# POOL masks the exponentials of a chunk-selected attention by an index select instead of a product with a triangle, under newly arranged lists

## The chip, the cores and the metric

The kernel runs on one core of one Trainium2 chip. The metric is the device time of one execution in microseconds, taken as the median of several runs. Engines are named as in the profile: PE (matrix products), DVE (vector), ACT (activation), POOL (GpSimd), SP (which here only issues DMAs).

## What is computed

Two steps in one program: attention in which each query looks only into the six best of its chunks of 32 keys, and then a two-layer network over all 3072 tokens. The reference, cut to what matters (B 4, H 8, S 768, D 64):

```python
k_min, k_max = min and max of k over each chunk of 32 keys
ub = sum(maximum(q * k_min, q * k_max), axis=-1)          # bound of a chunk, per query
ub = where(query's chunk >= chunk, ub, -1e9)
top_chunks = argsort(ub)[..., -6:]
mask = (key's chunk in top_chunks) & (query >= key)       # causal inside the chunks too
attn = softmax(where(mask, q @ k.T / sqrt(D), -1e9))
x = (attn @ v) as (3072, 512)
h = x @ w_in                                              # 512 -> 2048
g = where(h > 0, h, exp(minimum(h, 0)) - 1)
out = g @ w_out                                           # 2048 -> 512
```

## The kernel before

The work is recorded first and emitted afterwards. Every step (`g.op(name, engines, emit, reads, writes)`) is recorded as an operation with the engines that may do it and a function that emits its instructions. There are 2118 recorded operations, of which 1948 are emitted. Then one written list, `ORDER`, says in which order they are emitted and on which engine: three characters an entry, the engine (P PE, A ACT, D DVE, G POOL, S SP) and two digits for the operation's number. A second list, `PLACES`, says for each buffer, when it first appears, which of its class's slots it gets. So each engine runs its own entries strictly in the list's order, and a reused slot makes its new writer wait for its old readers. SP's entries are the DMAs, and these too are issued strictly in order.

The work comes in units of one batch and one half of the sequence (384 queries), eight in all; the first two units are built from the first and second quarter tiles of batches 0 and 1 together. In each unit, for each of four pairs of heads (`r`):

- `prep`: q and k are loaded (`ldk`, `ldq`), transposed on PE (`kT`, `qT`, line 543, line 402 for the paired units), copied out of PSUM (`kt`, `qt`) and into the operands of the score product (`ka`, `qa`); v is cast (`v`); chunk minima and maxima go to `kst`. For batches 2 and 3, and in the kernel's list these steps lie inside the work of earlier units, minima and maxima come from a contiguous load `ldc` into the one buffer `kc` (lines 480 to 501), and the k rows come transposed by DMA (`kd`). For batches 0 and 1 chunk-row indicators (`ec`) are copied by DMA from `econst` into the score operand.
- `select`: the bounds `ub` on PE (line 592), then on DVE transpose, largest eight, compare, transpose (lines 603 to 620), and `mk` copies the resulting rows into the operand, so that the score product itself adds a large negative number to keys of chunks that were not chosen.
- `attend`: for each step of key blocks a score product `sc` (line 782), the exponential `ex` on ACT (lines 797 and 801) into `pt`, and for the block or blocks on the diagonal the causal mask `tri` (line 814) on DVE or POOL. Then the products with v, `pv` (line 833), whose operand has a column of ones for the sum; `rcp` and `on` (lines 636 and 646) divide; the result is transposed (`px` on PE, line 669, and `xt`; or `xd` by DMA for batches 2 and 3) into `xt`, the network's input.
- `mlp`: for each of 16 blocks of 128 hidden columns a product `h` (line 851), `e` (exponential, ACT, line 858), `m` (minus one, POOL or DVE, line 860), `g` (maximum and minimum, DVE, line 864); then for each tile of 128 tokens 16 products into `o` (line 875, 893 for the last tile), a copy `oe` and the store `out`.

The list weaves the network of one unit between the attention of later ones. The weights w_in and w_out are loaded and cast to bf16 by POOL's DMA queue (`w_in0` to `w_in2`, `w_out0` to `w_out3`).

The causal mask before is one product a step. The `tri` tile holds ones on and above the diagonal; a step whose packed exponentials hold two diagonal blocks (at columns 0 and 384 of 512) is masked by one instruction over both:

```python
view = ap(pt)[:, :, PAD:PAD + 512].rearrange("p h (x w) -> p h x w", w=P)[:, :, ::3, :]
```

Here `h` is the two heads of the pair, so a single block is 128 x 256 elements, a double one 128 x 512, in bf16. There are 48 such masks, 18 on POOL and 30 on DVE; another 8, of line 740, belong to the paired units and are not touched.

Of the kernel before, what the change touches and what calls it, by code (L numbers as in the profile page):

```python
# [9 lines left out]
AOT = mybir.AluOpType  # L10
# [34 lines left out]
Pm-Pn6G2EAn7GbsGmGPn2Gn8D2pG2rAm+Dn0D14D0GAn3Dn4P2wPmWA2xA2yS2RP2JA2KDn5D2zPmSPmODn9Dn1AmXAmTD2L  # L45
GmYPnaGmHDmZAmPP3lAnbGmIA2FDmQDmUPmKAmLDmVD3nD3mA2MD3pGncPnGG2HPniA2AG07GmMA1fPnCG2SAnjD3oPnuD3q
D3rPnmDmRDmNG3tPneAnHA3sGnkDndAnvGnIP3HDnlAnDPnqGnwA3IDnJP41PnyDnxAnrA3uGnEDnFP3JP3+AnfPnQDnsS2k
A3KDntD2NAnnS3fG3LP2XA42P38PnRS2mA40GmJAnzA2GDnoD2ZDnpD2YP4lGngPnKPnXA4mD3vDnhA2+A30D43D3cP4DA4E
P4FG3ePnYA4GGnAD3aA3dD39D2-D31P4jD4HP3gG3bP33PnSS32S4+A34D35PnLA3hA4kD3iG3kS2TDnBP3wD4nS2VG2lG36
D3xG3jS50PnZPn-A2nD3yD3zA37S4-D3APnMPnTD3BD3CS4YD3GA3EG3FP3NDnUP4OP4MS4XS4ZP3MD3DP48P45A4PA4NP44  # L50
G2UG2WP4aD3ODn+D3PP4IP4JA4bP3SPnNA49D46D47A3TD4cS7UP3QD4QAnOP4sP4uP4dA3RP4eP4oS7SA4tP4pD4fP5rG3U
D4gA4vP4RD4KD4LP4SP4hA5sP5QS7WD4TD4UP3VP3WA5RD4qP5fP4VD3XD3YA5gS7RP5ED4rG4wP4xA4WP4yD5SP3ZA5FD4z
P58D4AA5iS57P5kD5aA4iP4BA4CG7VS53P5JD3-P5xD59G5TG5uA5cS55D5BA5oA5NPolPoJD5mA5GD5KPo5S5wAoKD5zS8l
PoxD5yGoLAo6SaND5LA5IPo9A5tDoMSo0G5bPodGo7AomD5lS51AoyG5MPohDo8G5nAoaSnPGonPoRA5OScZGobDooAoePoF
D7TA5hGofAoSPopDocG5AA5jGozDogPo1AoGGoTSnVDoAAoqPoBGoHDoUS7NAoiGorA5DPotDoIS7OAo2GojDosP5VAouGo3
DokA5HGovDo4A5UG5PDowA5vPoNAoCG5dD5XPp1A52G7XD5WAoOD5ZGoDPp2A5qGoPA5eD5YPpePpfD5-SnWPp7D5+SaHPp8
DoEA60G61DoQPpgD63A56DaOP66P6gA67P64DaQP6cP6iA65Pp3D62A6dDaPA6jP6mP68A6hP6lD5pP6aDaRP6eA6nPp9A69
D54SaSG6oA6fP6BP6xD6kPoVA6bS7MA6CP6vA6yS7YP6qA6wP6HS7PP6pAoWP6zA6IS7QPoZD6rGoXD6sA6AG5CP6JDoYAo-
P6tScRP6MGbmP6ND6uA6KP7bGo+P7cP76A6OP6-Dp0PphA77D6LA7dD6PShFScXG7eDaTP6FA6+Pp4ApiA6GP6DA6EP72P70
P78P6RDp5A71A79DaUP6QDaVA73P7CP74A75P6YA6ZP7xP7zA7yA7ADaWP7ZD7aD6SSb3P6WA6XPpaApbP7DSpjSp6G7BP8g  # L60
A8hD7-D81D6TD7+P7rP7lP7fP7gP7tP89P7pD8iA7EG7FD7hD7iD8aD8bG8kG8jP7vP8yD8zA7mA7sA7qA7uP7nA7oA7wP8m
# [24 lines left out]
AgbGgeDfODfVDghDfPSt9St3SrNPtCAtDGtEDtFPtuAgcAtvGtwAgsDtxPtaPtOAtbDtcDtdDfWPtqAfJAtrPtKGtsPu2AtL
AgtGtMGfXDttDtNAu3Gu4Du5AtPPtGPteAtHGtIAgrAfKAtfDtQDtRPfYAf+PtSPtyAtzAgiPtiGtgGtADfZAf-DthDtJPtm
AtnDtBDg0PtWAtjGgdAhWPt-AtTDtoPguGtkAt+Pu6DtpDtlPugPuhPuaDgwDtUDgyAtXAu7Gu8DtVPubPucDgvDgxGu0GtY
DgzDgAAgBAhUGgEDgDDu9DtZSg9PgLPgKAgMGgNPh7PhbPhaAhcPhpPgHPhoAhqAgIDu1PudPgFAgGPh5Ah8Ah6PhjPuiDgC
PgTPgYDgJAhkDhrPgVPhlAgUAhmPgPPgOPujDhdDh9PhfDgQDgRSgSAgWDhnPheDhgPgZDhhShiPi0PhXPhtPhsPi5Ag-Gg+  # L90
AueDgXAhYGh-DhuDhvPumAi6ShwAi1Gi4Di2Ph0Ph1Dh2PunAi7AhZPiaDh3Sh4Gh+Ai9PuoPupDicDibDieDidAuqAukPuQ
AuRGuSSulDifDigPuAAuBGuCPuIAuJDuKPuUPvoAvpAuVPuwGihAijPusAutDuDDuTDuLDuWGvqDvrPinAioPv0Av1PipGuu
PvcAiqAvdPv4DuXDuvDv2Av5GveDiiDv3DvfPjnPixPuYAuxGuyDuzAi3Gv6AiyAuZGu-PuEAuFPv8Av9Dv7PvkPirPuMGva
GuGAjoGikDu+DvbPvgPiDPiCAisAvlAuNDuHPizAiADuODuPPjlPiZAi-AvhPvyAjmPivAiwPvzPilPitAiuAiEGi8DvmGvi
DvjDvnPiTPiVPvAPj0Pj1PiXGiBDjpDiFPjLAimPiHPiGAiYAj2Gj3PjNPiPPiRPvBDiIDiJSiKAiUAiQAiSAiWAjMPjjPiL
AiMPjfPiNPvsDvCDi+Pj4AiOPj5PjrPjqPjbPj9Dj6PvtDj7Sj8SvDSufAjOAjgAjkSurPjdPjQAjcAjsAjaDjtPjRPjJPjh
PjFPjHPjzAjePjvAjiPjDPjuAjSAjKDjTPjBPvuPvEDjwDjxSjyAjIGjPAjAAjGAjEPjUAjCPjVDjWDjXSjYPvFPvvPvGPvH
DvIDvwPw6Aw7SvxPvKAvLGvMDvNSvJPwiPwuAwjAwvDwkPwqAwrDwwDw8Dw9PvSAvTGvUDwxPwaAwbDwcPweAwfPvOAvPDvV
DwlDwdGwgDwhPvWPwyGwsAvXDvQDvRGvYDvZPwGAwHPv-Av+DwtPw2GwIDwJAw3Dw4Dw5AwzDwAGw0Dw1PwKPwmPwQAwnGwo
DwpPwCAwDDwBPwRPwLPwSGwEDwFPwTAwUPwWPwXSwVPwMPwNDwOSwPPwYPwZAw-Sw+Px0Px1Px2Px3Dx4Sx5  # L100
"""
PLACES = """
012034567000812349a10562170103125110304017213233236458001721210034522131062120134456670324031011
2206007710050120112732140001224010263151400156000721281724932a00b64251ac1657102d30416e1437016309
223320f7043021311530628670152106220237123570a012142314310170156221021410330734530246020122041411
013220372g200316321192405302051640201701721225027311081cd5200002060406e9021430755723752601238153
71a120352101a27121432721b45240261757316202501312710500222315406030127270151364570450234567133110
045730800100f1302342252100616503a6472041131c24207710421802d5206301120214061921022e0g1512910a0145
2674031512743523a1241775162980451201421035041167265316730002002101672513725103406117231167213000
2313012501308020721366023010b6a8035241c104173002d2600401535341270021110020f001272602002315310e01  # L110
61242021924655001a2670213436574570014300947225611670302352031120804001116121g0720201135240126206
7b02263110d23604056a1340210e012f31211457500812314c3642415207730642056120013310460542957032603134
12613204502065601021112331061123044022301072011211a322032100236151720be0251232130061652720cg4100
0322251114847000022f1000017526231070952110345652110402506256200211162113123763020110222115100013
621710d340284051210226c02002a42311b212011506072123ef6420g301574113727512575374606247001012055473
# [865 lines left out]
```

## Time and profile before

| what | value |
| --- | --- |
| median of 3 runs | 281.3 us (280.84 to 281.32) |
| the profiled execution's own time | 281.25 us |
| its span, first to last instruction | 279.5 us |
| busy: PE | 263.2 us (94%) |
| busy: DVE, ACT | 217.4 us, 217.1 us (78% each) |
| busy: POOL | 125.5 us (45%) |
| moved by DMA | 38.47 MB |
| granted PE clock | 0.999 |

The span is what the profile shows; the execution's time is 1.7 us longer. Busy times are sums over the span and say nothing of when an engine was full; the profile can be cut into stretches for that. The ends of PE's products are modelled, so that a PE shown as busy throughout may still have short holes. A wait is put down to the one that came last. The groups of instructions give line, engine, operation, written and read tiles, shapes and count, then busy time, the mean of one instruction in ns, and the idle time ahead of them with what ended it.

### The profile page before, as it was taken

The numbers are of one execution on the slowest core, as the hardware profiler recorded it, in microseconds if no ns is written. First come the engines' busy times: TensorE is split into PE (matmuls) and PEld (weight loads), VectorE is DVE, ScalarE is ACT, GpSimd is POOL, SyncE is SP. The second block draws the span as 40 slices with busy tenths as digits, with TensorE's granted clock in tenths as the row PEclk, the third lists the DMA queues.
The fourth block names the chain that finished last, engine by engine and source line by source line (L and its number), as shares of the span: only waits on it lengthen the run. The fifth ranks groups of instructions, "written<-read, shape, count | busy, mean of one in ns | idle before, by whom it ended". The sixth has DMA issues, their size and how long they took to land.

```text
span 279.5 us, 6918 instructions
## 1 busy us (share of the span) xinstructions
PE 263.2 (94%) x2436; PEld 162.9 (58%) x2436; DVE 217.4 (78%) x656; ACT 217.1 (78%) x493; POOL 125.5 (45%) x249
## 2 busy tenths in 40 slices
PE   1978899999999999999999999999999999999994
PEld 0745465785456755576555555666655556665553
DVE  4668978799978999979998999569797698424931
ACT  2596796789699998999999859886968579982620
POOL 8674745348521755422685736222541346310410
PEclk9999999999999999999999999999999999999999
DMA  8999999999529999946985499416600210042002
GB/s 163 198 211 211 199 211 210 217 202 251 123 60 203 247 219 230 196 115 112 171 203 114 109 226 206 84 36 136 170 4 0 60 39 1 16 139 82 15 17 96
DMA packets 103779, 38.47 MB, mean 138 GB/s; under 512 B 95168, under 2 KB 99520, under 8 KB 103744
## 3 DMA queue, kind: packets, MB, share of 16 engines
q1 hardware_dynamic: 98864, 33.53, 57.3%
q0 software_dynamic: 3696, 4.19, 8.7%
q10 hardware_dynamic: 1184, 0.30, 0.5%
q8 instruction: 19, 0.31, 0.5%
q14 instruction: 16, 0.13, 0.1%
HBM read 30.41 MB, written 6.29 MB: 131 GB/s over the span
## 4 chain that ended last, share of the span: by engine, by line
PE 70%; DVE 13%; DMA 8%; ACT 4%; issue 1%; POOL 1%; SPq 0%; DVEq 0%; ACTq 0%
PE bank L875 24%; PE bank L851 22%; PE bank L782 9%; DMA w_in_sb<-in_moe_w_in_dram 5%; PE bank L833 5%; DVE gT L864 2%; PE bank L592 2%; PE bank L402 2%; DMA kc<-in_k_dram 2%; ACT e L858 2%; DMA f<-in_k_dram 1%; PE bank L543 1%; PE bank L728 1%; PE bank L893 1%; DVE on L646 1%
## 5 line engine op out<-in xcount | busy, mean ns | idle before, releaser
L851 PE MATMUL bank<-xt,w_in_sb 128*128 128x384 bf16 x512 | 89.2, 326 | 2.2 <-DMA w_in_sb<-in_moe_w_in_dram 2.2
L875 PE MATMUL bank<-w_out_sb,gT 128*128 128x512 bf16 x368 | 89.5, 379 | 0.0
L860 POOL TENSOR_SCALAR m<-e 128x384 f32<-128x384 f32 x96 | 50.7, 536 | 59.3 <-ACT e L858 47.0
L864 DVE SCALAR_TENSOR_TENSOR gT<-bank,m 128x384 bf16<-128x384 f32 x128 | 65.9, 549 | 9.7 <-POOL m L860 8.4
L858 ACT ACTIVATE e<-bank 128x384 f32<-128x384 f32 x128 | 58.6, 493 | 16.7 <-PE bank L851 13.9
L851 PEld LDWEIGHTS <-w_in_sb 128*128 128x128 bf16 x512 | 49.1, 98 | 36.6 <-DMA w_in_sb<-in_moe_w_in_dram 3.0
L797 ACT ACTIVATE pt<-bank 128x384 bf16<-128x384 f32 (+1 forms) x144 | 67.0, 547 | 3.5 <-PE bank L782 2.1
L875 PEld LDWEIGHTS <-gT 128*128 128x128 bf16 x368 | 34.6, 97 | 35.7 <-issue 2.2
L782 PE MATMUL bank<-rhs,lhs 96*128 96x384 bf16 (+2 forms) x240 | 42.8, 293 | 1.0 <-DVE on L646 0.5
L814 POOL TENSOR_TENSOR pt<-pt,tri 128x256 bf16<-128x256 bf16 (+1 forms) x18 | 16.6, 924 | 39.3 <-ACT pt L801 20.1
L782 PEld LDWEIGHTS <-lhs 96*128 96x128 bf16 x240 | 21.7, 97 | 13.9 <-issue 0.9
L833 PEld LDWEIGHTS <-pt 128*128 128x128 bf16 x576 | 21.0, 97 | 4.0 <-DVE pt L814 0.4
L833 PE MATMUL bank<-vext,pt 128*128 128x65 bf16 x576 | 22.2, 193 | 0.3 <-DVE pt L814 0.3
L646 DVE TENSOR_TENSOR on<-bank,rcp 128x384 bf16<-128x384 f32 (+1 forms) x37 | 18.8, 509 | 1.2
L367 DVE TENSOR_REDUCE kst<-bank 128x12 f32<-128x384 f32 x32 | 16.6, 548 | 3.7 <-PE bank L402 2.8
L322 POOL CAST rhs<-qt 64x384 bf16<-64x384 f32 x23 | 12.3, 542 | 13.1 <-ACT qt L320 12.1
L636 DVE RECIPROCAL rcp<-bank 128x6 f32<-128x6 f32 (+1 forms) x40 | 7.3, 185 | 14.0 <-PE bank L833 8.7
L320 ACT ACTIVATE o<-bank 128x512 f32<-128x512 f32 (+1 forms) x13 | 7.5, 587 | 13.0 <-PE bank L875 10.1
L322 DVE COPY o<-bank 128x512 f32<-128x512 f32 (+1 forms) x12 | 7.9, 663 | 12.0 <-PE bank L875 10.0
L860 DVE TENSOR_SCALAR m<-e 128x384 f32<-128x384 f32 x32 | 13.1, 417 | 2.8 <-ACT e L858 2.6
L402 PE MATMUL bank<-ident_f,f 96*128 96x96 f32 x64 | 9.3, 295 | 6.2 <-DMA f<-in_k_dram 6.2
L814 DVE TENSOR_TENSOR pt<-pt,tri 128x512 bf16<-128x512 bf16 (+1 forms) x30 | 10.8, 376 | 5.3 <-ACT pt L801 3.5
(102 smaller groups left out, 338.6 us busy)
## 6 DMA issues: line engine op xcount, KB each, us to landing
f<-in_v_dram SPq DMA_DIRECT2D x22, 256.0 KB, 4.8
out_dram<-o SPq DMA_DIRECT2D x21, 256.0 KB, 3.4
f<-in_q_dram SPq DMA_DIRECT2D x18, 256.0 KB, 4.9
f<-in_k_dram SPq DMA_DIRECT2D x18, 256.0 KB, 4.7
kc<-in_k_dram SPq DMA_DIRECT2D x8, 384.0 KB, 4.3
w_out_sb<-in_moe_w_out_dram POOLq DMA_DIRECT2D x4, 512.0 KB, 10.5
f<-in_q_dram SPq DMA_DIRECT2D x6, 192.0 KB, 5.0
w_in_sb<-in_moe_w_in_dram POOLq DMA_DIRECT2D x2, 512.0 KB, 8.8
```

Of the source, the lines that this page charges most:

```text
L322: eng[e].tensor_copy(out=dst, in_=src)
L367: g.op(("kmin", "kmax")[w] + tag, (DVE,), lambda e, w=w, op=op: nc.vector.tensor_reduce(out=cs(w), in_=src(), axis=AX.X, op=op), reads=[(b ...
L646: nc.vector.tensor_tensor(out=ap(on)[:, 0:nt].rearrange("p q h d -> p h q d"), in0=view()[:, :, :, 0:D], in1=ap(rcp)[:, :, 0:nt].to_broadc ...
L782: nc.tensor.matmul(ap(banks[hd])[:, o + pc:o + pc + wd], lhsT=apl(ls, G)[0:96, pr, hd, P * kb:P * (kb + 1)], rhs=ap(rs)[0:96, hd, c0 - HS ...
L797: lambda e, hd=hd, pt=pt, banks=banks, wtot=wtot: nc.scalar.activation(out=ap(pt)[:, hd, PAD:PAD + wtot], in_=ap(banks[hd])[:, 0:wtot], fu ...
L814: eng[e].tensor_tensor(out=view, in0=view, in1=tri[:, 64:64 + P].rearrange("p (a b w) -> p a b w", a=1, b=1) .to_broadcast([P, 2, len(dg), ...
L833: nc.tensor.matmul(view()[:, hd, qi, :], lhsT=ap(pt)[:, hd, P * qi + off:P * qi + off + P], rhs=ap(vx[b])[:, kb, 2 * r + hd, :], start=(kb ...
L851: nc.tensor.matmul(ap(bank)[:, 0:HS], lhsT=w_in_sb[:, kk, P * fc:P * (fc + 1)], rhs=ap(xT[i, kk]), start=(kk == 0), stop=(kk == NKK - 1))
L858: g.op(f"e{i}.{fc}", (ACT,), lambda e, eb=eb, bank=bank: nc.scalar.activation(out=ap(eb), in_=ap(bank)[:, 0:HS], func=AF.Exp), reads=[(ban ...
L860: g.op(f"m{i}.{fc}", (POOL, DVE), lambda e, eb=eb, mb=mb: eng[e].tensor_scalar(out=ap(mb), in0=ap(eb), scalar1=-1.0, scalar2=1.0, op0=AOT. ...
L864: nc.vector.scalar_tensor_tensor(out=ap(gt), in0=ap(bank)[:, 0:HS], scalar=0.0, in1=ap(mb), op0=AOT.max, op1=AOT.min),
L875: nc.tensor.matmul(ap(bank), lhsT=ap(gts[fc])[:, P * tt:P * (tt + 1)], rhs=w_out_sb[:, fc, :], start=(fc == 0), stop=(fc == NFC - 1))
```

## The change

In `mask`, where the engine is POOL, each diagonal block of the two heads is masked by `affine_select`: elements whose query index is at or above the key's partition are kept, others become zero. The triangle isn't read there. A step with two diagonal blocks takes two instructions. On DVE the product with the triangle stays.

```diff
                 def mask(e, pt=pt, dg=dg):
+                    if e == POOL:
+                        for pc in dg:
+                            part = ap(pt)[:, :, PAD + pc:PAD + pc + P]
+                            nc.gpsimd.affine_select(out=part, in_=part, compare_op=AOT.is_ge, fill=0.0, base=0,
+                                                    pattern=[[0, 2], [1, P]], channel_multiplier=-1)
+                        return
                     if len(dg) == 2:
```

Both lists are written anew. The first 126 entries are the same but for the place of a few among engines that do not depend on each other; each engine's own order is the same up to there. Behind them the entries of each engine are in another order in many places, 53 operations go to another engine of those allowed, and buffers get other slots. The first, the fourth and the fifth row of the list:

```diff
-G0iS0WD01A02D09D06S0sG0kD0jG0aS0yD03D00D0qG0mG0bA0VG04D05G0eS0uG0cG0dA0tS0rS0vS0xD0lD0oS0wS0YS0X
+D01A02G0iS0WD09D06S0sG0kD0jG0aS0yD03D00D0qG0mG0bA0VG04D05G0eS0uG0cG0dA0tS0rS0vS0xD0lD0oS0wS0YS0X
...
-P1DP26P25P1ED10G0-S2PS2vS2OD27D28D1FA1wP1YP20P2aGmDA0SP29D2bP1XA2cP1+D21G0JP1IP1OP1RP1SP1HS2IP2o
-P1ND1GD1JD1ZD1KP2dG1dGmFA1-P1LD2qD1PA1QD2jD22P23D1TD1UD2eA2sD24A1MS2QP1VD1WG08G2uG0hP2BD2DD2CA2t
...
+P1DP26P25P1ED10G0-S2PS2vS2OD27D28D1FA1wP1YP20P2aGmDA0SP29D2bP1XA2cP1+D21G0JP1IP1OP1RP1SP1HS2kS2I
+P2oP1ND1GD1JD1ZD1KP2dG1dGmFA1-P1LD2qD1PA1QD2jD22P23D1TD1UD2eA2sD24A1MS2QP1VD1WG08G2uG0hP2BD2DD2CA2t
...
```

What goes to another engine, by count: of the 48 masks of `attend` one goes from DVE to POOL (`tri0113`) and one from POOL to DVE (`tri2011`), so 18 and 30 stay; one mask of a paired unit goes from DVE to POOL (`tri1s1`). ACT gives seven copies of q rows (`qa`) and takes three of the paired units, three `ky` and some others; DVE takes three casts of v and gives up two `m`, two `mk` and a few copies of k. Counts of the network's products, of the DMAs and of PE's instructions are the same.

More of the change, by code (lines that the diff above doesn't have):

```diff
@@ L50 @@
[L50 to L61, printed above, removed]
@@ new lines @@
+AmTGmYDmZPnaGmHAmPDmQGmIA2FG2HP3lD3nD3mD3pD3oGmUDmVA1fAnbA2APmKAmLG07GncGmMA2MG2SPnGPnCAnHPniAnj
+PnuAnvD3qD3rG3tA3sDndDmRDmNPnePnmP3HGnkGnwGnIDnlAnDPnqA3IPnyDnxDnJAnrAnfA3uGnEDnFP3+P3JPnQDnsDnt
+A3KG3LD2NAnnS2VS2mS4-P2XD2ZP41A42PnKPnRA40GmJD3vDnoDnpP4lGngDnhPnXA2+AnzA2GP4DA4mD2YA30D31D43D2-
+P38D3cA4EP4FGnAP4jPnYA4GD3aA3dD39G3bG3eA4kD4HP33P3gPnLPnSA34D35A3hA2lA3kA3jD3iP3wDnBD3xD3yD3zD3A
+D3BA37D3CG3GPnZPnMPnTDnUD3FPn-Dn+A36A2nP3NP4JP3MS3fP4OP4IP4MA3DA4PG3ES32P4aP48D3OD3PD4nA4bA49G2W
+S2TG2UP44G4cP3SP45P3QA3TD46D47D4KD4LA4ND4QPnNP4sP4pP4oP4uA3RAnOA4vA4tP4eP4dD4fS4+P4RP4SS50P5fP5r
@@ new lines @@
+A5sD4gP4hP5QD4qD5gA4iG3UP3WP3VP5ED4TD4UA5RA5tP4VA4WG4wP4xP4yA5SD3XD3YP3ZS4YS4ZS4XP58P5kD4rD4zD4A
+P4BA4CD3-D5aD5uP5xD5zA5FD5yG5AP5JD5LD5KA5NA5cPolAomS7UG7VPoJPo5Po9S7WS7QSaNS7SS55S53S57SaHS51S5w
+So0SnPSaCS7RD5lD59GonDooD5mA5BAoKGoLA5oDoMD5GG5MA5hAo6Go7AoaDo8D7TGobG5nG5bDocPodAoeGofDogA5iA5T
+PopPoxAoyPoRAoSA5OGozDoAGoTDoUPoFAoGGoHDoIPohAoqGorDosPoBPo1AoiGojDokAo2Go3Do4A5IPotAouG5HG5jGov
+P5VD5WD5XDowD5YD5ZD5-D5+PoNPp7Pp8PpePp1PpfPp2AoCA5eA5DA5dAoOG5pGoDDoEPpgA5UA7XA5PGoPDoQA52A60D54
+G5qG5vP66A67P6gP68P6cP6lP6mPp9P6iA6hA6dA6nA69A6jP64P6aA65A6bPp3P6eA6fG61P6BP6xA6yPoVA6CDaOD5CD56
@@ new lines @@
+DaPDaRD6kD62G6oP6vP6pP6HP6qP6zDaQD63A6wAoWA6IPoZD6rD6sA6AP6JP6tGoXDoYD6uAo-Go+Dp0A6KP7cP7bA7dP6M
+P6NA6OD6PS7YS7PSaSS7NS8lS7MDaTDaUP76A77PphP70A71P6FA6GApiP78P6DA6EP6-Pp4Dp5P72DaWG6LP6RG7eP6QA79
+A6+A73P6WP74A75P7xP7rA7sA6XP6YA6ZP7zPpaA7ySnWS7OP7ZD7aDaVD6SD6TScRSnVSb3ScXSc+A7AP7CP8gA8hP7pA7q
+P7DP7fP7tP7gG7BD7+D7-G80D81G82D8iA7uA7EP7lP7vA7wP7nA7oP6UA7mA6VP89A8dP8yA8CP8mA8qG7FP7HG8kD7hD7i
+D8aD8bSpjDb4Sp6SaDP7GD7ID7JG8EG8fP8tP7jP84P8FA7kApbG8jG8sA8uA8DA8vD8zP7KD7LPpEPpMPpQPpAD8AD8GDb5
+D8eD8oD8nApFGpGDpHG8BA85ApRDboGpSDpTA86G8pScZAaIA8HPpsD8rDaYApNDpODpPPpkPpIG8cP8KGbmAplGpmDpnD8M
@@ L101 @@
+PwCAwDDwBPwQPwRPwLPwSGwEDwFPwTAwUPwWPwXSwVPwMPwNDwOSwPPwYPwZAw-Sw+Px0Px1Px2Px3Dx4Sx5
 """
 PLACES = """
[L103 to L107, printed above, removed]
@@ L118 @@
+325516162011
 """
```

106 lines of the change are left out of this document (52 added, 54 removed).

## The prediction

> **What bounds the kernel now.** I read the page's first two parts, then busy time by stretches, then the waits of PE in the one stretch where it is idle, then the groups of the masks. The page's head and the chain that ended last:
>
> ```profile
> span 279.5 us, 6918 instructions
> PE 263.2 (94%) x2436; PEld 162.9 (58%) x2436; DVE 217.4 (78%) x656; ACT 217.1 (78%) x493; POOL 125.5 (45%) x249
> PE 70%; DVE 13%; DMA 8%; ACT 4%; issue 1%; POOL 1%; SPq 0%; DVEq 0%; ACTq 0%
> ```
>
> PE sets the end, and POOL, whose work the code change shortens, is 1% of the chain. An average hides where the 16.3 us of idle PE lie; the stretches tell it (columns: stretch, length, then busy us of each engine, the granted clock, the DMA share and GB/s):
>
> ```profile
> 0.00:40.00 40.00, 29.28 (x274) 19.45 (x275) 27.86 (x88) 26.38 (x63) 25.89 (x73) 1.00 1.19 197
> 40.00:80.00 40.00, 40.00 (x392) 24.82 (x391) 36.03 (x121) 32.29 (x72) 20.21 (x40) 1.00 0.89 187
> 80.00:150.00 70.00, 67.93 (x678) 43.32 (x677) 63.36 (x189) 66.77 (x157) 34.63 (x66) 1.00 0.85 175
> 150.00:270.00 120.00, 120.00 (x1055) 71.29 (x1053) 88.99 (x260) 90.71 (x203) 44.80 (x73) 1.00 0.36 84
> 270.00:279.50 9.50, 5.97 (x44) 4.04 (x42) 1.12 (x2) 0.98 (x2) 0.00 (x0) 0.98 0.23 83
> ```
>
> Idle PE: 10.7 us in the first 40 us (loads), none from 40 to 80, 2.07 us from 80 to 150, none from 150 to 270, 3.5 us behind the last product. From 80 to 150 ACT is busy 95% and DVE 91% of the time: three engines are close to full there, and nowhere else. So a new order of the same work can win some two microseconds in the middle, or lose more; the two ends are outside its reach unless the early transfers move. What PE waited for from 80 to 150:
>
> ```profile
> PE bank L669 <- DVE on L646: 0.8, 2, 0.5
> PE bank L782 <- DVE on L646: 0.5, 1, 0.5
> PE bank L782 <- ACT rhs L320: 0.5, 1, 0.5
> PE bank L833 <- DVE pt L814: 0.3, 1, 0.3
> ```
>
> These four make the 2.07 us: 1.6 named for DVE, 0.5 for ACT, none for POOL. The L669 ones are the transposes px013 and px113, which wait for `on013` and `on113` on DVE; the L833 one is the first pv product, waiting for a DVE mask.
>
> **The masks.** Eighteen of the 48 masks of `attend` are on POOL; the edit replaces each by one index select a diagonal block.
>
> ```profile
> L814 POOL TENSOR_TENSOR pt<-pt,tri 128x256 bf16<-128x256 bf16 x11 | 8.3, 755 | 25.7 <-ACT pt L801 20.1 <-DMA lhs<-kt 3.4 <-PE bank L833 2.2
> L814 POOL TENSOR_TENSOR pt<-pt,tri 128x512 bf16<-128x512 bf16 x7 | 8.3, 1190 | 13.6 <-ACT pt L797 12.6 <-PE bank L833 1.0
> L263 POOL TENSOR_SCALAR_AFFINE_SELECT tri<-tri 128x128 bf16<-128x128 bf16 x1 | 0.3, 291 | 0.1
> L268 POOL TENSOR_SCALAR_AFFINE_SELECT trineg<-trineg 128x128 bf16<-128x128 bf16 x1 | 0.4, 396 | 0.0
> L268 POOL TENSOR_SCALAR_AFFINE_SELECT trineg<-trineg 128x384 bf16<-128x384 bf16 x1 | 0.5, 512 | 0.0
> L276 POOL TENSOR_SCALAR_AFFINE_SELECT econst<-econst 32x384 bf16<-32x384 bf16 x2 | 1.1, 580 | 0.1
> ```
>
> No select of 128x256 stands in the trace. The nearest are L268, also two blocks side by side: 396 ns for 128 elements, 512 for 384, so 0.45 us for 256 on their line. The ends are 0.29 (L263) and 0.58 (L276). A single-block mask goes from 0.755 to 0.45; a two-block mask becomes two selects, 1.19 to 0.90. Sum over 11 and 7: 16.6 to 11 x 0.45 + 14 x 0.45 = 11.3 us, 5.3 us off POOL. At 0.29 it would be 9.3 us off, at 0.58 still 2.1 us off. After the new lists POOL keeps 18 masks here (one comes from DVE, one goes), so the sum stands.
>
> On the path this is worth nothing by itself. No row of PE's waits names POOL's mask, in the whole run; POOL sat idle 39.3 us ahead of its masks, waiting for the exponential of ACT. What hides it is the PE work between the last score product and the pv products. If that cover were gone, each mask would be worth 0.3 us.
>
> A shorter mask could matter through the port. The DVE mask below ran inside POOL's two-block masks and took 0.55 us, against a mean of 0.31 for its form:
>
> ```profile
> 154.28 2.53 POOL L814 TENSOR_TENSOR pt<-pt,tri 128x512 bf16<-128x512 bf16 x2 [1.00 <-PE bank L833]
> 155.25 0.55 DVE L814 TENSOR_TENSOR pt<-pt,tri 128x256 bf16<-128x256 bf16 x1
> L814 DVE TENSOR_TENSOR pt<-pt,tri 128x256 bf16<-128x256 bf16 x13 | 3.9, 308 | 3.7 <-ACT pt L801 3.5
> ```
>
> So POOL and DVE masks do slow each other, 0.24 us in this pair. I count nothing for it in the forecast: 0.31 is the usual price, so overlaps are few. The Trainium skill, "SBUF — State Buffer", section on the two separate sides, says that a GpSimd instruction and a DVE one with two SBUF inputs hold one shared port pair by turns, each for its whole length; this pair of rows agrees. By that rule every microsecond taken off POOL's masks could come back to DVE, which is the third rival.
>
> **The lists.** Both lists hold the same 1948 operations; behind the first loads nearly all positions and many buffer places differ. Totals hardly move: by the group means DVE loses 0.1 and ACT 0.5 us over the run. What moves is where the work lies, so I counted each engine's list up to the instruction that PE waits for.
>
> ```profile
> L860 DVE TENSOR_SCALAR m<-e 128x384 f32<-128x384 f32 x32 | 13.1, 417 | 2.8 <-ACT e L858 2.6
> L322 DVE COPY rhs<-selT 32x768 bf16<-32x768 bf16 x7 | 2.5, 353 | 0.2
> L322 DVE COPY lhs<-kt 64x384 bf16<-64x384 bf16 x5 | 1.5, 309 | 0.0
> L322 DVE CAST kt<-bank 128x384 bf16<-128x384 f32 x4 | 2.2, 550 | 0.0
> L322 DVE CAST vext<-f 128x512 bf16<-128x512 f32 x4 | 1.7, 424 | 0.0
> L320 ACT ACTIVATE rhs<-qt 64x384 bf16<-64x384 f32 x28 | 14.2, 518 | 0.5
> ```
>
> - DVE up to `on013`: 187 instructions of its list before, 183 after. Ten go (kinds of 0.31 to 0.55 us: `m0.2`, copies of k rows and masks) and six come (`v012` at 0.42, a copy of q and others). By kind that is 1.5 us less; four at 0.31 to 0.55 bound it by 1.2 and 2.2.
> - DVE up to `on113`: 259 against 251 operations, 2.3 us less by kind (8 x 0.31 = 2.5 is the near bound).
> - ACT up to the last exponential of the unit of batch 0, second half (`ex01331`): 149 against 154, so 5 x 0.52 = 2.6 us more. Up to the mask row copy `mk201`, which the last wait of the four is for: 278 against 274, 2.1 us less.
>
> So DVE comes to both transposes 1.5 to 2.3 us earlier by its own list, against waits of 0.4 us each. ACT is loaded earlier: 2.6 us more ahead of 90 us, where it has 7.7 us idle from 40 to 80, and 4.7 us less between 90 and 148, where it had 3.2 us idle in 70. All four waits are in reach. PE's own list is the same at the two transposes (position 211 and 298 in both), so the cover in front of them is unchanged.
>
> What is late next: behind an `on` that comes in time stand the score products whose exponentials ACT must do, one ACT instruction (0.52 us) behind. I take half of the 2.07 us as won, 1.0 us. Ends: 2.1 us won, or nothing.
>
> **The early transfers.** SP's list changes from its 22nd entry on, and that queue is full early: two q loads took 6.41 us to issue, one chunk-row copy 8.67 us.
>
> ```profile
> 18.05 6.41 SPq L304 DMA_DIRECT2D f<-in_q_dram  x2
> 26.27 8.67 SPq L304 DMA_DIRECT2D lhs<-econst  x1
> 18.06 13.64 DMA w_in_sb<-in_moe_w_in_dram
> 31.75 4.07 PE bank L851 x24
> w_in_sb<-in_moe_w_in_dram POOLq DMA_DIRECT2D x1, 1024.0 KB, 13.6
> ```
>
> The last w_in piece lands in the same crowd and PE starts on it at 31.75. The new list puts a v load ahead of one chunk-row copy and two v loads and a q load ahead of the next ones; by entry 33 the same transfers are out. The neighbours of w_in are other packets, not more. I take 0, with 1 us either way (PE idles up to 10.7 us in that stretch, so it can go both ways), and keep it for the range.
>
> **Sum.** Masks 0, port 0, lists -1.0, early transfers 0. The profiled execution took 281.25 us, 1.7 above its span and within 0.05 of the median 281.3; span 278.5, time 280.2.
>
> **Rivals.**
>
> *Slower: the k loads of batch 1 come late.* The k rows that kT110 transposes are loaded by three transfers. Before, two of them went out long ahead and one stood behind the kc load; now all three stand behind it, together with a chunk-row copy and a store, and the kc load waits until DVE is through with the one kc buffer.
>
> ```profile
> 79.47 1.18 DVE L493 TENSOR_TENSOR kc<-kc 96x256 f32<-96x256 f32 x2
> 80.68 0.22 DVE L493 TENSOR_TENSOR km<-kc 96x64 f32<-96x64 f32 x1
> 80.93 0.33 SPq L304 DMA_DIRECT2D kc<-in_k_dram  x1
> 81.31 0.42 SPq L304 DMA_DIRECT2D f<-in_k_dram  x1
> 81.79 0.67 SPq L304 DMA_DIRECT2D lhs<-econst  x1
> 89.39 0.50 PE L543 MATMUL bank<-ident_f,f 128*128 128x128 f32 x3
> f<-in_k_dram SPq DMA_DIRECT2D x18, 256.0 KB, 4.7
> ```
>
> Issued at the old time the six would take 0.33 + 3 x 0.42 + 0.67 and a store, some 3 us, and 4.7 us to land: 88.7, or 90.5 if five transfers at once share the 175 GB/s of that stretch. PE needs them at 89.4 plus 1.1 us, as its list has that much more ahead of kT110. DVE's list to the end of the kc work is three operations shorter (157 against 154, some 1.3 us). So it holds unless DVE comes over 1.5 us later than by its list, or the transfers land 3 us late. Then PE stands behind kT110, with DVE's reductions and ACT's copies behind that: 1 to 3 us, 282.2 to 284. For it: PE, ACT and DVE are all near full there. Against it: the sum just made. Chance 0.30, with other late transfers of this queue counted here, as they go by the same mechanism.
>
> *No change.* DVE's gain is eaten by ACT, which now does 2.6 us more up to `ex01331` in a stretch (80 to 90) where it has almost no idle time; the waits change their names, 281.3. Selects that run at 0.755 us in the crowded stretch, so that the mask edit does not do what it says, end here too. Chance 0.20.
>
> *The port.* The same stretches for POOL's masks alone:
>
> ```profile
> 80.00:150.00 70.00, 5.05 (x7) 1.00 0.85 175
> ```
>
> Seven of them lie from 80 to 150, 5.05 us. At 0.3 us less each, 2.1 us of port time would come back to DVE exactly where it is near full; all four waits go and the rest of ACT's comes with them: 2.1 us off plus 0.5 for weight loads that start earlier, 278.7. One pair with 0.24 us speaks for it; the mean of 0.31 over all 13 masks of that form, so near the shortest, speaks against. Chance 0.08.
>
> **How the numbers follow.** Forecast 0.42, port 0.08, no change 0.20, slower 0.30. About 0.2% (0.56 us) is what a measurement of this kernel can tell from no change. Forecast and port are faster: 0.50; 0.20 the same; 0.30 slower. The range takes the forecast's ends (279.1 to 281.3), the port's price nearly whole at 278.8, and of the slower case all up to 282.8, leaving out its upper part (0.12) and the early transfers' far ends.
>
> **What would show it.** Right: the selects of POOL at 0.40 to 0.50 us; PE's waits of 80 to 150 under 1.5 us with fewer for `on` (L646); PE idle in the first 40 us within 0.5 us of 10.7; ACT busier before 90 and less after. Wrong: a PE wait on f loaded from k near 90 us, selects at 0.6 us or more, waits of PE for POOL's masks, or a later start on w_in's last piece than 31.75.

## The result and the profile after

The changed kernel takes 283.18 us (median of 7 runs, 281.88 to 284.07) against 281.3 us before (7 runs, 280.42 to 282.05): ratio 1.0064, 95% interval 1.0045 to 1.0083. It is 0.64% slower. The prediction said 280.2 us and a range up to 282.8.

The profiled execution took 284.07 us. Head and chain of the page after:

```profile
span 282.4 us, 6929 instructions
PE 265.5 (94%) x2436; PEld 163.6 (58%) x2436; DVE 213.8 (76%) x652; ACT 216.9 (77%) x494; POOL 122.2 (43%) x260
PE 75%; DVE 11%; DMA 7%; ACT 2%; issue 2%; POOL 1%; SPq 1%; DVEq 0%; ACTq 0%
```

DVE was busy 3.6 us less than before and POOL 3.3 us less, and the span is 2.9 us longer. PE has as many instructions as before; its busy time is 2.3 us longer. In part that is short holes which the modelled ends hide; in part PE's granted clock, which was 0.50 for 6.8 us of this execution, from 21.4 us on (before it was 1.00 there):

```profile
22.00:24.00 2.00, 1.19 (x4) 0.58 (x5) 1.39 (x3) 0.00 (x0) 1.06 (x4) 0.50 1.22 197
```

The clock is not what makes the kernel slower: of the seven executions, the one with a mean clock of 1.00 took 283.26 us. So no engine has more to do; the order of the work costs the time, as the experiments show. The selects, from the groups of instructions after:

```profile
L812 POOL TENSOR_SCALAR_AFFINE_SELECT pt<-pt 128x256 bf16<-128x256 bf16 x26 | 10.8, 433 | 41.8 <-ACT pt L801 22.1
```

26 selects of 0.433 us, 10.8 us in all: the step foretold with 0.45 and 11.3 us. Busy time by stretches after (same columns as before):

```profile
0.00:40.00 40.00, 30.20 (x270) 19.97 (x271) 26.60 (x86) 25.96 (x62) 25.82 (x73) 0.91 1.19 198
40.00:80.00 40.00, 39.35 (x384) 24.13 (x383) 34.69 (x115) 32.11 (x71) 19.44 (x38) 1.00 0.93 180
80.00:150.00 70.00, 67.61 (x678) 43.14 (x677) 61.40 (x181) 63.90 (x155) 37.25 (x74) 1.00 0.86 168
150.00:270.00 120.00, 119.52 (x1053) 71.11 (x1051) 88.73 (x269) 93.94 (x208) 39.29 (x78) 1.00 0.40 90
```

From 40 to 80 PE was never idle before and loses 0.65 us now, and PE, DVE and ACT all get through less there than before (384 products against 392). What PE waited for from 80 to 150, after:

```profile
PE bank L669 <- DVE on L646: 2.1, 2, 1.1
PE bank L543 <- ACT xt L320: 0.3, 1, 0.3
```

These are the two transposes of the prediction, px013 and px113. Their waits did not shrink from 0.8 us; they grew to 2.1.

Counting PE's instructions along the list gives the start of each step (where a product is missing in the records, its weight load places it). Start in the kernel before, and the difference of the others, in us; the mended kernels are those of the first and the second study below:

| step on PE | before | after | first place mended | both places | both, two kc buffers |
| --- | --- | --- | --- | --- | --- |
| h0.15 (last w_in piece) | 31.75 | +0.47 | +0.09 | -0.77 | +0.57 |
| ub01 | 68.43 | +1.51 | -0.09 | -0.96 | +0.38 |
| px013 | 97.04 | +2.58 | +0.42 | -2.10 | -0.75 |
| px113 | 133.16 | +2.93 | +0.78 | -2.23 | -1.64 |
| h5.7 | 195.50 | +2.78 | +0.59 | -1.90 | -1.99 |
| last product | 275.38 | +2.79 | +0.80 | -1.95 | -1.87 |

The first row holds what the early loads and the lower clock near 22 us did in that one execution. Below it, the changed kernel loses 1.0 us up to ub01 and 1.1 between ub01 and px013; between px013 and px113 it gains and loses alike.

**The first place, 59 to 72 us.** ACT's timeline after and then before, around the copies of k out of PSUM (`kt`), with the idle time in brackets:

```profile
60.10 0.48 ACT L320 ACTIVATE qt<-bank 128x384 f32<-128x384 f32 x1
62.20 0.87 ACT L320 ACTIVATE kt<-bank 128x384 bf16<-128x384 f32 x2 [1.61 <-DVE kst L367]
...
65.19 0.49 ACT L320 ACTIVATE kt<-bank 128x384 bf16<-128x384 f32 x1 [0.97 <-DVE kst L367]
```

```profile
60.20 1.25 ACT L320 ACTIVATE kt<-bank 128x384 bf16<-128x384 f32 x3 [0.25 <-DVE kst L367]
```

Before, ACT copies three k tiles in a row. After, it stands 1.61 and 0.97 us for DVE's chunk extrema. The two do not need each other's results: both read the same bank, which PE's transpose kT has filled. But in these rows a bank that two engines read is read in the order in which the list names them, one wholly behind the other. The new list names `kmax013`, `kmin013` (DVE) ahead of `kt013` (ACT): `kmin013`, the row below, ends at 62.10 and `kt013` starts at 62.20.

```profile
61.56 0.54 DVE L367 TENSOR_REDUCE kst<-bank 128x12 f32<-128x384 f32 x1
```

It names `kt010` ahead of `kmin010`, and so DVE then waits for ACT:

```profile
63.10 0.56 DVE L367 TENSOR_REDUCE kst<-bank 128x12 f32<-128x384 f32 x1 [0.53 <-ACT kt L320]
64.08 0.56 DVE L870 SCALAR_TENSOR_TENSOR gT<-bank,m 128x384 bf16<-128x384 f32 x1 [0.42 <-POOL m L866]
```

The second row is `g1.5`, late because its exponential stood on ACT behind `kt010`. Behind `g1.5` on DVE stands `kmax011`, and for that `kt011` waits on ACT (the 0.97). The network's banks come free late, and PE stalls 0.2 to 0.4 us at each of five products from 62 to 71.

**The second place, 95 to 99 us.** DVE's timeline after, then before:

```profile
96.95 1.02 DVE L367 TENSOR_REDUCE kst<-bank 128x12 f32<-128x384 f32 x2 [1.74 <-ACT kt L320]
```

```profile
93.37 1.48 DVE L367 TENSOR_REDUCE kst<-bank 128x12 f32<-128x384 f32 x3
```

Before, `kmin111` and `kmax111` read their bank first and `kt111` followed. Now `kt111` is first, and on ACT exponentials and copies stand ahead of it without a gap: it comes only at 96.37. DVE, whose own list is four entries shorter up to `on013`, stands 1.74 us until it has ended, and `on013` comes late to px013.

```profile
96.37 0.55 ACT L320 ACTIVATE kt<-bank 128x384 bf16<-128x384 f32 x1
```

**The third place, 126 to 136 us.** DVE's timeline after:

```profile
130.96 0.69 DVE L484 TENSOR_TENSOR kn<-kc 96x512 f32<-96x512 f32 x1 [1.69 <-DMA kc<-in_k_dram]
```

There is one `kc` buffer. DVE frees it at 125.5 us, the next load is issued at once (125.57), and DVE has too little else in its list until it lands. `on113` ends at 136.04 and px113 waits 1.1 us.

The Trainium skill, "PSUM — Partial Sum Buffer", section "PSUM bank collisions raise a hardware error", says that two engines must not touch the same bank in the same 32 partitions at once, reads against reads included, and that the compiler's scheduler adds a dependency between two such instructions. The 62.10 and 62.20 above agree. No run here shows what reading at once would do.

### The profile page after: what moved, and what is told of

It is laid out like the page before. It is cut to its first block, busy times and chain, and to the rows that moved or that the text cites. A ratio compares the mean times of both kernels' runs of the same rounds, so it can differ in the third digit from the quotient of the medians.

```text
span 282.4 us, 6929 instructions
## 1 busy us (share of the span) xinstructions
PE 265.5 (94%) x2436; PEld 163.6 (58%) x2436; DVE 213.8 (76%) x652; ACT 216.9 (77%) x494; POOL 122.2 (43%) x260
## 3 DMA queue, kind: packets, MB, share of 16 engines
q0 software_dynamic: 3696, 4.19, 8.7%
## 4 chain that ended last, share of the span: by engine, by line
PE 75%; DVE 11%; DMA 7%; ACT 2%; issue 2%; POOL 1%; SPq 1%; DVEq 0%; ACTq 0%
PE bank L857 28%; PE bank L881 23%; PE bank L782 9%; PE bank L839 4%; DMA w_in_sb<-in_moe_w_in_dram 3%; PE bank L592 2%; PE bank L543 2%; DMA kc<-in_k_dram 2%; DVE kst L367 2%; DVE gT L870 2%; DVE on L646 2%; DMA f<-in_k_dram 2%; PE bank L402 1%; PE bank L728 1%; PE bank L899 1%
## 5 line engine op out<-in xcount | busy, mean ns | idle before, releaser
L857 PE MATMUL bank<-xt,w_in_sb 128*128 128x384 bf16 x512 | 92.1, 332 | 2.1 <-DMA w_in_sb<-in_moe_w_in_dram 1.0
L866 POOL TENSOR_SCALAR m<-e 128x384 f32<-128x384 f32 x98 | 51.5, 536 | 55.3 <-ACT e L864 41.9
L857 PEld LDWEIGHTS <-w_in_sb 128*128 128x128 bf16 x512 | 50.0, 99 | 38.3 <-issue 6.9
L797 ACT ACTIVATE pt<-bank 128x384 bf16<-128x384 f32 (+1 forms) x144 | 66.1, 546 | 2.9 <-PE bank L782 1.6
L812 POOL TENSOR_SCALAR_AFFINE_SELECT pt<-pt 128x256 bf16<-128x256 bf16 x26 | 10.8, 433 | 41.8 <-ACT pt L801 22.1
L322 POOL CAST rhs<-qt 64x384 bf16<-64x384 f32 x24 | 13.2, 555 | 12.4 <-ACT qt L320 11.9
L322 DVE COPY o<-bank 128x512 f32<-128x512 f32 (+1 forms) x13 | 8.7, 666 | 11.5 <-PE bank L881 9.5
L866 DVE TENSOR_SCALAR m<-e 128x384 f32<-128x384 f32 x30 | 11.7, 395 | 5.0 <-ACT e L864 4.5
L801 ACT ACTIVATE pt<-bank 128x512 bf16<-128x512 f32 x24 | 13.9, 605 | 1.7 <-PE bank L782 1.0
```

Of the source, the lines that this page charges most:

```text
L322: eng[e].tensor_copy(out=dst, in_=src)
L797: lambda e, hd=hd, pt=pt, banks=banks, wtot=wtot: nc.scalar.activation(out=ap(pt)[:, hd, PAD:PAD + wtot], in_=ap(banks[hd])[:, 0:wtot], fu ...
L801: g.op(f"ex{tag}{si}", (ACT,), lambda e, pt=pt, banks=banks: nc.scalar.activation(out=ap(pt)[:, :, PAD:PAD + 256], in_=ap(banks[0])[:, :]. ...
L857: nc.tensor.matmul(ap(bank)[:, 0:HS], lhsT=w_in_sb[:, kk, P * fc:P * (fc + 1)], rhs=ap(xT[i, kk]), start=(kk == 0), stop=(kk == NKK - 1))
L866: g.op(f"m{i}.{fc}", (POOL, DVE), lambda e, eb=eb, mb=mb: eng[e].tensor_scalar(out=ap(mb), in0=ap(eb), scalar1=-1.0, scalar2=1.0, op0=AOT. ...
```

## Experiments

All ratios are against the kernel before, run on the same chip in the same call, with 95% intervals.

**First study: which half of the change, and the two places.** The selects with the lists of before, and the new lists with the product:

```diff
-ORDER, PLACES of the changed kernel        # selects alone
+ORDER, PLACES of the kernel before
```

> The lists of before with the index select on POOL: the 18 masks at 0.43 us a block instead of 0.755 and 1.19 us. Theory 'lists' (all of the loss comes from the new lists, the select hides in POOL's idle time): the same as before, 281.3, within 0.5 us; POOL busy 5 us less. Rival 'select' (the select holds something that DVE needs, or comes late for the products with v): 282 to 283.

281.16 us, 0.9985 [0.9964, 1.0006]: not different from before.

```diff
-                    if e == POOL:            # new lists alone
-                        for pc in dg:
...
```

> The lists of after with the triangle product on POOL as before. Theory 'lists': as slow as after, 283.2, or up to 0.5 us slower. Rival 'select': back to 281.3.

283.4 us, 1.0067 [1.0043, 1.0091], as the changed kernel. The loss is the lists'.

Then two kernels with the whole change, where each engine's own order stays as it is and only the place of a few ACT entries in the common list moves (five in the first, three in the second), so that only the order across engines, in which a bank is read, changes:

```diff
-... kmax013 kmin013 kt013 kt010 ... kmax011 kt012 e1.11 m1.11 kt011
+... kt013 kt010 kmax013 kmin013 ... kt012 e1.11 kt011 kmax011 m1.11
```

> After, with each engine's own order untouched; only the places of six ACT entries between the engines change: the copies kt013, kt010, kt011 stand ahead of the reductions kmax013, kmin013, kmax011 of the same bank. Theory 'bank order' (a PSUM bank that ACT and DVE both read is read in the list's order, so ACT waits at 61 to 65 us for DVE's reductions, DVE then for ACT and POOL, and PE for the banks): the stalls of PE from 62 to 72 us, 1.4 us together, go, and the time falls by 1.0 to 1.6 us, to about 281.9. Rival 'early loads' (the loss is the PE clock that falls to 0.5 near 22 us and the w_in loads): no change, 283.2.

281.62 us, 1.0006 [0.9988, 1.0024]. Of PE's waits from 40 to 150 us only those for `on` and the small one for `xt` are left:

```profile
PE bank L669 <- DVE on L646: 2.1, 2, 1.1
PE bank L543 <- ACT xt L320: 0.3, 1, 0.3
```

```diff
-... kT111 kt111 kT113 kt113 kT112 kt112 ... kmin111 kmax111
+... kT111 kT113 kT112 ... kmin111 kmax111 kt111 kt113 kt112
```

> After, again with each engine's own order untouched: the copies kt111, kt113, kt112 of ACT stand behind the reductions kmin111 and kmax111. Theory 'bank order': DVE no longer idles 1.7 us ahead of kmin111 at 95 us, on013 comes 1.0 to 1.7 us earlier, PE's waits at qT113 and px013 (0.48 and 1.18 us) shrink to under 0.7 together; time 0.7 to 1.2 us less than after, about 282.2, if nothing further on takes it back. Rival 'ACT is full' (ACT's 2.6 us more of work up to there are what is late): no change, 283.2. Rival 'early loads': 283.2.

282.08 us, 1.0022 [1.0005, 1.0039]. Now the waits for `on` are nearly gone and those of the first place are left:

```profile
PE bank L857 <- DVE gT L870: 0.9, 3, 0.5
PE bank L669 <- DVE on L646: 0.2, 1, 0.2
```

So 1.6 us hang on the first place and 1.1 on the second, with no engine's list changed.

**Second study: do they add, what is left, and the reverse.** Both places:

> The changed kernel with both mended places of its list at once: `kt013, kt010` ahead of `kmax013` and `kt012, e1.11, kt011` ahead of `kmax011` (59 to 72 us), and `kt111, kt113, kt112` behind `kmax111` (95 to 99 us). Each engine's own order stays that of the changed kernel. Theory (the order in which ACT and DVE read one PSUM bank): the two are apart by 25 us, so the gains of the two alone, 1.6 and 1.1 us from 283.2, mostly add: 280.4 to 281.0, and no wait of PE at h1.6 to h1.12 nor over 0.4 us at qT113; what is left of the loss is at px113 and behind 160 us. Rival (one rank behind the other: an engine that comes early at the first place runs into the next wait, the kc load at 126 us): no better than the first alone, 281.6.

280.02 us, 0.9951 [0.9932, 0.9970], better than either and a little better than expected. Against the lists of before with the same selects (0.9985 [0.9964, 1.0006]) that is 0.34%, 1.0 us: once the two places are mended, the new lists are the faster ones, as far as two intervals that just overlap can tell. One wait of PE over 0.2 us is left from 40 to 150 us, and another behind it, at the first product that needs `xd203`:

```profile
PE bank L669 <- DVE on L646: 0.6, 1, 0.6
```

```profile
PE bank L857 <- DMA xt<-on: 0.8, 1, 0.8
```

The second is SP's queue. In the new list `ldc301`, which waits for DVE, stands ahead of three others, and the DMA transpose `kd300` goes out right behind all four. Before, only `ldc301` went out right ahead of it. Its issue before and in this kernel:

```profile
149.46 1.23 SPq L467 DMA_TRANSPOSE lhs<-kt  x1
```

```profile
148.65 4.89 SPq L467 DMA_TRANSPOSE lhs<-kt  x1
153.59 0.59 SPq L304 DMA_DIRECT2D f<-in_k_dram  x1
154.22 0.58 SPq L304 DMA_DIRECT2D out_dram<-o  x1
154.90 5.11 SPq L657 DMA_TRANSPOSE xt<-on  x4
```

The `xd` transposes wait behind its 4.89 us. So the three were put first:

```diff
-ldc301 ldk302 out2.1.0 ldk311 kd300
+ldk302 out2.1.0 ldk311 ldc301 kd300
```

> As the run before, and on SP's queue the three issues ldk302, out2.1.0 and ldk311 stand ahead of ldc301, which waits for DVE. Theory (the DMA transpose kd300 takes 4.5 us to issue because the loads held up behind ldc301 go out right ahead of it, and the transposes xd200 to xd203 stand behind it): kd300 issues in about 1.2 us as in the kernel before, xd203 goes out near 160 us, the wait of PE at h4.8 (0.6 to 1.0) is gone: 0.5 to 1.0 us below the run before, 279.6 to 280.3. Rival (the transpose is slow for what runs beside it in the DMA engines, not for its place): kd300 still over 4 us and the time as the run before.

279.72 us, 0.9934 [0.9914, 0.9953]. The issue is short again, and PE's wait for `xt` is gone. So the place in the queue made the issue long. In time little came of it: the 0.3 us in the median, where 0.5 to 1.0 were expected, lie within the intervals.

```profile
147.86 1.23 SPq L467 DMA_TRANSPOSE lhs<-kt  x1
```

Then two `kc` buffers, in place of the SP order:

```diff
-BUFS = dict(f=11, kc=1, ... thr=2, selb=2, selT=2, ...
+BUFS = dict(f=11, kc=2, ... thr=1, selb=1, selT=1, ...
```

> As the first run, and the contiguous k load has two buffers instead of one (thr, selb and selT have one each instead of two, to make room). Theory (DVE, ahead of its old time, waits 1.7 us for the one kc buffer's load at 129 to 131 us, and SP's queue stands behind the same buffer at 150 us): the wait ahead of kminc211a goes, PE's stall at px113 falls from 1.3 to 0.4 us or less, kd300 issues early: 0.8 to 1.6 us below the first run, 279.0 to 280.0. Rival (DVE's place at px113 is set by its own work, or the single thr, selb and selT make new waits at the selects): px113 as before and the time at or above the first run.

278.72 us, 0.9896 [0.9878, 0.9915], the fastest of all, 1.0% under the kernel before and a little under the 279.0 to 280.0 expected. Of PE's waits from 40 to 270 us this is all that the profile names:

```profile
PE bank L881 <- issue: 0.2, 1, 0.2
```

And the kernel before, made worse in the same way: only the place of `kmin111`, `kmax111` and three DVE entries behind them, now behind ACT's `kt111`:

```diff
-... kmin111 kmax111 ... kmin113 ... kminc210a kt113 ka0113 ... kt111
+... kt113 ... kt111 kmin111 kmax111 kmin113 kminc210a ka0113 ...
```

> The kernel before, products with the triangle and all, with every engine's own order untouched; only in the list across engines kmin111, kmax111, kmin113 and the two DVE entries behind them stand behind ACT's kt111, as they do in the changed kernel. Theory (a bank that two engines read is read in the list's order): DVE waits 1.5 to 2.7 us for kt111 near 95 us, on013 comes as much later, PE stalls at px013 by 1.5 to 2.5 us instead of 0.7; some of it is regained behind 130 us: 282.0 to 283.3. Rival (reads of a bank are free of each other and only the engines' own orders count): 281.2, as the kernel before, on013 at its old time.

285.55 us, 1.0148 [1.0128, 1.0167]: the direction as expected, the size twice that. DVE's timeline and PE's waits there:

```profile
96.23 1.49 DVE L367 TENSOR_REDUCE kst<-bank 128x12 f32<-128x384 f32 x3 [2.69 <-ACT kt L320]
```

```profile
PE bank L669 <- DVE on L646: 3.3, 2, 3.0
```

px013 is 2.52 us late, as expected. The rest came with PE's clock, which the expectation did not have. PE has stood for 2.97 us, and 1.1 us after px013 its granted clock falls to 0.50, for 3.41 us:

```profile
101.00:102.00 1.00, 1.00 (x5) 0.47 (x4) 1.00 (x5) 0.55 (x3) 0.00 (x0) 0.50 0.86 181
```

In the kernel before it is 1.00 there. The products of h2.8 start 0.32 us apart instead of 0.16, those of h2.2 and h2.7 likewise, which makes 1.7 us more, so that ub11 is 4.19 us late, and nothing is regained up to the end (+4.26). All five executions of this kernel have the same mean clock, 0.988. So the order of the reads itself cost 2.5 us here, and the clock behind the long stand the other 1.7.

**Third study: the kc buffer alone, and the masks again.** The changed kernel with two `kc` buffers and nothing mended:

> The changed kernel with its own list, and two buffers for the contiguous k load instead of one (thr, selb and selT one each instead of two). The ring of bank reads at 59 to 72 us and the wait of kmin111 at 95 us stay. Theory (the late places add up, each with its own price): only what happens behind 125 us goes, the 1.3 us at px113 (0.4 without it) and the late kd300 with 0.6 us at h4.8: 1.0 to 1.6 us below the changed kernel's 283.2, 281.6 to 282.3. Rival (the kc load is late only because the engines came to it out of step after 60 us, so with the rings left in place the second buffer is worth nothing): 283.2.

282.17 us, 1.0014 [0.9997, 1.0031]; by ratio 0.5% or 1.4 us better than the changed kernel. The three places add: 0.58, 0.42 and 0.50% one by one make 1.50%, and all three together are 1.68% (1.0064 to 0.9896).

The selects on the lists of before, with two `kc` buffers:

> The lists of the kernel before with the index select on POOL, and the contiguous k load with two buffers instead of one (thr, selb and selT one each). Theory (the one kc buffer binds only where DVE comes early, and with the lists of before it hardly waits for it, 0.3 us in all between 80 and 170 us): no change against the kernel before, 280.9 to 281.4. Rival (the second buffer is a gain of its own, whatever the lists): 1 us or more faster, 279.5 to 280.3, and the gain of the mended lists with two buffers would then be put down to the buffer.

280.73 us, 0.9968 [0.9955, 0.9982]. That is between the two: 0.3% under before, but not told apart from the selects with one buffer (0.9985 [0.9964, 1.0006]). There the second buffer brings 0.17%, 0.5 us, if anything, and 1.4 us with the new lists. It also settles what the lists are worth: with selects and two buffers on both, the mended lists (0.9896) are 0.72%, 2.0 us, faster than those of before, well outside the intervals.

The fastest version with the product on POOL instead of selects:

> The fastest version so far, both places of the list mended and two buffers for the k load, but POOL multiplies with the triangle again (0.76 and 1.19 us) instead of selecting. Theory (POOL's masks lie behind PE's work and the port they share with DVE costs little): same as that version within 0.3 us, 278.5 to 279.0. Rival (once the waits are gone DVE sets the end of both transposes, and every mask that runs beside a DVE instruction delays it): 0.6 to 1.5 us slower, 279.3 to 280.2.

279.91 us, 0.9940 [0.9923, 0.9957]: 1.2 us slower than with selects. My theory fell. With the waits gone the masks do count. DVE from 153 us and POOL's masks beside it, in this kernel:

```profile
153.08 1.18 DVE L484 TENSOR_TENSOR kn<-kc 96x512 f32<-96x512 f32 x1
155.78 2.07 DVE L487 TENSOR_TENSOR kc<-kc 96x512 f32<-96x512 f32 x1
```

```profile
152.51 2.77 POOL L814 TENSOR_TENSOR pt<-pt,tri 128x512 bf16<-128x512 bf16 x2 [3.33 <-ACT pt L797]
155.22 0.49 POOL L322 CAST rhs<-qt 64x384 bf16<-64x384 f32 x1
155.67 0.60 POOL L322 CAST kt<-f 128x512 bf16<-128x512 f32 x1
```

and in the fastest version with selects:

```profile
152.74 0.78 DVE L484 TENSOR_TENSOR kn<-kc 96x512 f32<-96x512 f32 x1
155.44 1.29 DVE L487 TENSOR_TENSOR kc<-kc 96x512 f32<-96x512 f32 x1
```

`kminc301a` takes 0.4 us longer beside the product. `kmaxc301a` takes 0.8 us longer beside the copies that POOL comes to only now. `on203` behind them is 1.1 us later than there, 0.3 of it from further ahead. Two explanations were open, the length of POOL's masks or the product's two inputs, and the last run doubles the length without the product:

```diff
-                        for pc in dg:
+                        for pc in dg + dg:
```

> The fastest version so far, with every index select on POOL issued twice (the second changes nothing in the data): 52 of 0.43 us, so POOL spends 0.87 us on a single block and 1.73 on a double one, more than the 0.76 and 1.19 of the products with the triangle. It tells apart why the products cost 1.2 us on the mended lists. Theory (the length of POOL's masks: they end later, and the copies behind them fall on other DVE work): at least as slow as with the products, 279.9 or more, and `kmaxc301a` again near 2 us. Rival (a product with two inputs in SBUF holds DVE up beside it, a select doesn't, however long): 278.5 to 279.0, as with single selects, and `kminc301a` at 0.8 us beside the selects where it took 1.18 beside the products.

280.16 us, 0.9959 [0.9945, 0.9973], as slow as with the product: the length theory, by the time. But its rows do not show what that theory had said:

```profile
152.47 3.43 POOL L812 TENSOR_SCALAR_AFFINE_SELECT pt<-pt 128x256 bf16<-128x256 bf16 x8 [2.98 <-ACT pt L797]
```

```profile
153.05 0.78 DVE L484 TENSOR_TENSOR kn<-kc 96x512 f32<-96x512 f32 x1
155.75 0.69 DVE L487 TENSOR_TENSOR kc<-kc 96x512 f32<-96x512 f32 x1
...
157.09 1.68 DVE L493 TENSOR_TENSOR kc<-kc 96x256 f32<-96x256 f32 x2
```

Beside eight selects back to back `kminc301a` takes the same 0.78 us; `kmaxc301a` is short where I had expected 2 us, and it is the next step, `kmaxc301b`, that falls beside POOL's copies and takes 1.68 us instead of 0.73. It would be wrong to read from this that a select leaves DVE alone and a product does not. With no POOL instruction under way when it begins, this form takes 0.69 us, so that 0.78 is 0.09 too much; and in the kernel with selects alone, one select in front of it is enough for 0.23:

```profile
129.25 0.69 DVE L484 TENSOR_TENSOR kn<-kc 96x512 f32<-96x512 f32 x1 [0.68 <-DMA kc<-in_k_dram]
129.97 0.92 DVE L487 TENSOR_TENSOR kc<-kc 96x512 f32<-96x512 f32 x1
```

```profile
129.94 0.41 POOL L812 TENSOR_SCALAR_AFFINE_SELECT pt<-pt 128x256 bf16<-128x256 bf16 x1 [3.21 <-ACT pt L801]
```

The excess goes by how much of the POOL instruction under way is left when DVE's begins. `kminc301a` meets a select that ends at 153.29, 0.24 us later, and takes 0.09 too much; here 0.38 us are left, and it is 0.23; beside the product, which ends at 153.71, 0.63 us are left, and it is 0.49. And POOL's next instruction waits in its turn. Of the eight selects, the one that begins inside `kminc301a` takes twice its 0.43 us:

```profile
153.25 0.85 POOL L812 TENSOR_SCALAR_AFFINE_SELECT pt<-pt 128x256 bf16<-128x256 bf16 x1
```

So with masks, what counts for this wait is the length of the single one that DVE meets, some 1.2 us for a product over two blocks and 0.41 for a select, however many follow. And every mask that ends later shifts POOL's copies onto other DVE work. Behind copies DVE waited longer: its 2.07 us at 155.78 in the kernel with products span three of them, and why these did not take turns with DVE is not shown. DVE's busy time over the whole run fits: 213.7 us with single selects, 217.4 with products and 216.1 with doubled selects, for the same 652 instructions. The doubled selects also made PE wait for a mask itself, 0.4 us once. How the 1.2 us of the product divide between the two effects was not measured.

## Why the prediction was wrong, point by point

- **The masks, 0 by themselves, selects 0.45 us.** The size held (0.433; 26 selects instead of 25, as the mask that comes from DVE has two blocks and the one that goes has one). That they are worth nothing held on the lists in question (283.4 with the product, 283.18 with selects), and failed on mended ones, where they bring 1.2 us.
- **The port, 0, as a rival 278.7.** Nothing on the changed lists. The rival's mechanism is there: DVE waits for the POOL instruction under way, and with the selects alone DVE is busy 215.7 us instead of 217.4. The larger waits hid it, and the time stayed the same (281.16). That the fastest kernel's 278.72 is the rival's number is luck; it has mended lists and a second buffer.
- **The lists, -1.0 us: the step that failed.** I counted each engine's work up to the instruction that PE waits for and found DVE 1.5 and 2.3 us ahead. What I left out is that an engine's list is not only its own. Where ACT and DVE read one bank, the common list also says who reads first, and at two places it put the engine that was free behind the one that was still busy. These cost 1.6 and 1.1 us. A list that is shorter in front of such a wait, or of the one `kc` buffer, buys idle time: DVE's two gains turned into 1.74 and 1.69 us of standing. The direction of the count was right: with the order of bank reads mended, the same engine orders are 1.0 us faster than those of before with the same selects. That this is just the forecast's 1.0 is luck, as the forecast had neither place in it.
- **"None from 40 to 80."** I took a stretch in which PE had no idle time for one in which nothing could be lost, and looked at order only from 80 to 150. The largest loss was there. Nor is it so that three engines are close to full "nowhere else": before the change, the ten microseconds around the first place were as full for PE, DVE and ACT, which the average over 40 us hid.

```profile
60.00:70.00 10.00, 10.00 (x86) 5.50 (x84) 9.18 (x20) 9.70 (x24) 6.71 (x16) 1.00 0.96 237
```
- **Early transfers, 0 within 1 us either way.** h0.15 starts at 32.23 instead of 31.75, and in the other kernels with these lists from 0.77 us earlier to 0.57 later: inside the bound, though the later start here was one of the signs named for being wrong.
- **The slower rival, k loads late at kT110.** It ended on the right side, by the wrong mechanism: no wait of PE for k appears near 90 us. **No change, the gain eaten by ACT:** close to what happens at the second place, where `kt111` stands behind ACT's exponentials; but I gave it the price of a gain lost and not that of a wait made.
- **The signs.** The selects came as said. PE's waits from 80 to 150 were 2.4 us and not under 1.5, PE's idle time in the first 40 us was 9.8 us and not within 0.5 of 10.7, and ACT was not busier before 90 us (68.0 us against 68.3), only less busy after. So the signs said that the gain had not come; none of them pointed at either place.

## What to carry to other kernels

Before counting what each engine has ahead of a wait, list the buffers that two engines read, and see which read the common order puts first: the reader with nothing to wait for should go first, as moving five entries past others, which changed no engine's own order, was worth 1.6 us here, and moving five the wrong way cost 4.1, some 1.7 of it by a lower clock behind the long stand of PE. When a loss is larger than the wait that should explain it, look at the granted clock in short stretches. Gains in front of a single-buffered load or of a queue that waits in order are only real if the load comes earlier too. And price an edit again after the larger waits are gone: the select was worth nothing at first and 1.2 us at the end.

## What the runs showed of the hardware

- A DVE instruction with two SBUF inputs, 96x512 in f32, took 0.69 us with no POOL instruction under way, 1.18 us behind a product on POOL, and 0.78 and 0.92 us behind a select. The excess went by what was left of that POOL instruction, and a select that began inside the DVE instruction took 0.85 us instead of 0.43. The Trainium skill, "SBUF — State Buffer", section "SBUF: two separate sides", states that such an instruction and a GpSimd one that reads SBUF hold a shared port pair by turns, each for its whole length. These rows agree, for the select as for the product; the 2.07 us behind three copies are more than one such turn.
- The issue of one DMA transpose took 1.23 us with one load issued right in front of it, and 4.54 to 4.89 us with four transfers issued right in front.
- Behind a stand of PE of 2.97 us the granted clock fell to 0.50 for 3.41 us, starting 1.1 us after PE had begun again. In the kernel with selects alone, stands of 1.69 and 1.77 us, near 26 and 32 us, were not followed by a fall. But in ten of the fourteen kernels profiled it also fell to 0.50 near 21 us, for 3.41 or 6.83 us, without a stand of PE over 1.5 us ahead of it other than at the start; so what makes it fall, no run here shows.
